# Tokens put in order by strided reads ahead of the first layer, and stores with 32 partitions as the outermost dimension

## The chip, the cores and the metric

The kernel runs on one core of one Trainium2 chip. The metric is the device time of one execution in microseconds (us). The engines are TensorE (PE in the rows; PEld is its weight load), VectorE (DVE), ScalarE (ACT), GpSimd (POOL) and SyncE (SP), whose queue issues most of the DMAs.

## What is computed

A causal convolution of 7 taps over the tokens, with softmaxed taps per head, and behind it two layers without attention: 192 to 2048 columns and back, with a squared ReLU in the first and a leaky ReLU in the second.

```python
def _attn_ref(x, weight):                      # x: 4 x 4096 x 192, weight: 8 heads x 7 taps
    ...
    w = np.exp(w)
    w = w / (np.sum(w, axis=-1, keepdims=True) + 1e-09)
    ...
    out = np.einsum('hk,bskhg->bshg', w, x_unf)
    return out.reshape(B, S, D)

def _moe_ref(x, w_in, w_out):                  # 16384 x 192, 192 x 2048, 2048 x 192
    h = x @ w_in
    r = np.maximum(h, 0.0)
    return (r * r) @ w_out

def _moe2_ref(x, w_in, w_out):
    h = x @ w_in
    return np.maximum(0.01 * h, h) @ w_out
```

## The kernel before

The 16384 tokens are cut into 32 tiles of TT = 512. A unit u = (l, t) is tile t in layer l; data stand with the 192 channels on partitions (a part "a" of 128 and a part "b" of 64) and the 512 tokens along the row. The units run in a fixed order: (1,0) to (1,3), (2,0), (2,1), and then alternately (2,t) and (1,t+2). Each unit has 8 steps. In a step TensorE makes two blocks of h (`g1`, from the operand x in X[u]) and, one step behind, multiplies the former step's blocks into the output o (`g2`). Every product is split into a high and a low part in fp32r for precision, so each block of h goes through ScalarE and VectorE: `act`, `most`, then `high` (line 385, ScalarE copy to fp32r) and `low` (line 389, VectorE subtraction), which make hi and lo, the moving operands of `g2`.

The operand x of a first-layer tile comes from the convolution. `load_x` (line 247) brings raw tokens from DRAM, `transpose` (line 267) turns blocks of 32 by 32, and `conv` sums the taps on VectorE into acc_a or acc_b in SBUF (lines 289 and 291); the first two tiles' part a is convolved on TensorE into PSUM (`conv_pe`, the name conv). Then four instructions split the result: `split_a` (line 326) and `split_b` (line 336) copy on ScalarE to the high part, `split_a_lo` (line 329) and `split_b_lo` (line 340) subtract on VectorE to the low part, and `copy_half` (line 320) copies halves between partitions with DMAs on SP's queue. The second layer's operand is split by the same four functions from the evacuated output z of layer one (`evac`, lines 425 to 433).

Each product (line 347) reads its moving operand in the order "p (a b) -> p b a" with a = 2: output column 2b + a is input column 256a + b. A tile passes four products, so its tokens stand in a turned order at the end: a column's 9-bit number has been rotated by 4 bits. The store undoes that. `store` (lines 447 to 457) transposes z in blocks of 32 by 32 into y_a or y_b and writes each group of 32 channels with one DMA of 512 runs of 32 floats (128 bytes), 65.5 KB. Its DRAM side has the order "(b i a) d -> a b i d" with b = 16, a = 2, so its outermost dimension has 2 elements, then 16, 16 and 32. The stores of all tiles go to SP's queue; for the last tile they alternate between SP's and ScalarE's.

What runs when is written out by hand (`tc.manual_schedule`). In each step `pieces` picks waiting instructions (the preparation of later tiles, the leaving of finished ones, the decoding of the int64-stored weights at lines 115 to 149) by due time and by a budget of costs in ns, which are constants in the code. On each engine the instructions then stay in that order. PSUM holds four blocks of h; X has four buffers, and the staging tiles w, y_a and y_b share three.

Of the kernel before, what the change touches and what calls it, by code (L numbers as in the profile page):

```python
# [31 lines left out]
def conv_moe_moe2_kernel(  # L32
# [20 lines left out]
    nc = tc.nc  # L53
# [21 lines left out]
    f32 = lambda ap: ap.bitcast(F32)  # L75
# [9 lines left out]
    for l in (1, 2):  # L85
        W[l] = dict(

            i=const.tile([P, NP, 3, 2, P], F32R, name=f"i{l}"),
# [218 lines left out]
    X, order, split = {}, [], set()  # L307

    def operand(u):
        if u not in X:  # L310
            X[u] = px.tile([P, 3, 2, TT], F32R, tag="x", name="x")
            order.append(u)
        return X[u]

    def room(u):

        return u in X or len(order) < XB or g1_left[order[len(order) - XB]] == 0

    def copy_half(u, k, to, k_from):
        nc.sync.dma_start(  # L320
            out=f32(X[u][halves(to), k].rearrange("p a t -> p (a t)")),
            in_=f32(X[u][halves(1 - to), k_from].rearrange("p a t -> p (a t)")),
        )

    def split_a(u, src):
        nc.scalar.copy(out=operand(u)[:, 0, 0, :], in_=src)  # L326

    def split_a_lo(u, src):
        nc.vector.tensor_sub(out=X[u][:, 0, 1, :], in0=src, in1=f32(X[u][:, 0, 0, :]))  # L329
        for i in range(2):  # L330
            copy_half(u, 1, i, 0)
        split.add(u)

    def split_b(u, src, half):
        v = halves(half)
        nc.scalar.copy(out=operand(u)[v, 2, 0, :], in_=src[v])  # L336

    def split_b_lo(u, src, half):
        v = halves(half)
        nc.vector.tensor_sub(out=X[u][v, 2, 1, :], in0=src[v], in1=f32(X[u][v, 2, 0, :]))  # L340
        copy_half(u, 2, 1 - half, 2)
        split.add(u)

# [73 lines left out]
    def evac(u):  # L417

        l, t = u
        o = ops.pop(u)  # L420
        z = {}

        def take(n, i):
            z[n, i] = pz.tile([P, HT], F32, tag="z", name="z")[:, 0:TT]
            (nc.vector.tensor_copy if i else nc.scalar.copy)(out=z[n, i], in_=o[n][i])  # L425

        def add(n):
            nc.vector.tensor_add(out=z[n, 0], in0=z[n, 0], in1=z[n, 1])  # L428
            if n == 1:
                nc.gpsimd.tensor_copy(out=z[1, 1][0:R], in_=z[1, 0][R:2 * R])  # L430

        def add_r():
            nc.vector.tensor_add(out=z[1, 0][0:R], in0=z[1, 0][0:R], in1=z[1, 1][0:R])  # L433

        now = [lambda n=n, i=i: take(n, i) for n in range(2) for i in range(2)]
        adds = [(690, lambda: add(1)), (690, lambda: add(0)), (690, add_r)]
        if l == 1:
            v = (2, t)
            free = lambda: room(v)
            return now, [z_ + (None,) for z_ in adds] + [  # L440
                (-600, lambda: split_a(v, z[0, 0]), free),
                (690, lambda: split_a_lo(v, z[0, 0]), free),
                (-600, lambda: split_b(v, z[1, 0], 0), free),
                (690, lambda: split_b_lo(v, z[1, 0], 0), free),
            ]

        def store(nm, src, n, dmas):
            y = stage.tile([P, TT], F32, tag="w", name=f"y_{nm}", bufs=WB)
            nc.vector.transpose(out=y[0:n], in_=src[0:n])
            d0 = 0 if nm == "a" else P  # L450

            for j in range(n // 32):
                to = out[t * TT:(t + 1) * TT, d0 + 32 * j:d0 + 32 * j + 32]
                dmas[j % len(dmas)].dma_start(  # L454
                    out=to.rearrange("(b i a) d -> a b i d", b=16, a=2),
                    in_=y[32 * j:32 * j + 32, :].rearrange("p (i d) -> p i d", d=32),
                )

        dmas = [nc.sync] if t < NT - 1 else [nc.sync, nc.scalar]
        both = adds + [  # L460
            (700, lambda: store("a", z[0, 0], P, dmas)),
            (700, lambda: store("b", z[1, 0], R, dmas)),
        ]
        if t == NT - 1:
            both = [both[i] for i in (1, 3, 0, 2, 4)]
        return now, [z_ + (None,) for z_ in both]
# [20 lines left out]
    with tc.manual_schedule():  # L487
# [67 lines left out]
        for i, (_, p) in enumerate(pieces):  # L555
            p()
            decode_ahead(400)
            if i == 2:
                xT1 = transpose_second()
        split_a((1, 0), acc0)  # L560
        split_a_lo((1, 0), acc0)
        split_b((1, 0), accb[0], 0)
        split_b_lo((1, 0), accb[0], 0)
        decode_ahead(10000)
        acc1 = conv_pe(xT1)

        def rest_of_second():
            split_b((1, 1), accb[0], 1)
            split_b_lo((1, 1), accb[0], 1)
            split_a((1, 1), acc1)  # L570
            split_a_lo((1, 1), acc1)
# [67 lines left out]
        for s in range(NS + 1):  # L639
            if s < NS:  # L640
                u, p = steps[s]
# [4 lines left out]
                if p == 0:  # L646
                    while u not in X or any(z[4] == u for z in list(prep) + list(leave)):
                        q = leave if any(z[4] == u for z in leave) else prep
                        z = q.popleft()
# [7 lines left out]
            if s:  # L657
                u2, p2 = steps[s - 1]
                g2(u2, p2)
                if p2 == NP - 1:  # L660
                    while leave:
                        z = leave.popleft()
# [76 lines left out]
```

## Time and profile before

| | us |
|---|---|
| median of 3 runs | 2244.81 (2244.11 to 2244.94) |
| profiled execution, its time | 2244.63 |
| profiled execution, its span | 2242.9 |
| TensorE busy | 2153.6 (96%) |
| VectorE busy | 1647.1 (73%) |
| ScalarE busy | 1657.9 (74%) |
| GpSimd busy | 83.7 (4%) |

The span is what the trace covers; the time of the execution is 1.73 us more. Busy times are sums over the instructions of an engine; a matmul's end is modelled, and weight loads run beside matmuls. In a row of a timeline the first number is the start in us from the span's start, the second the duration, and brackets hold the idle time before the instruction and what ended it. A DMA row on SPq or ACTq is the time for which the issuing queue was held, not the transfer.

### The profile page before, as it was taken

The page shows a single profiled execution, that of the slowest core. Times are in us where ns is not written, and L with a number is a line of the kernel's source. Part 1 is how long each engine was busy: PE and PEld are TensorE (multiplying, and loading weights), DVE is VectorE, ACT ScalarE, POOL GpSimd, SP SyncE. Part 2 cuts the span into 40 slices and gives each one's busy share as a digit, 9 for nine tenths or more (in the row PEclk, how much of TensorE's full clock was granted, in tenths as well). Part 3 has the DMA queues.
Part 4 walks back from the last instruction along what each step waited for, and adds up shares of the span by engine and source line. Part 5 has one row for each costly group of instructions (what it writes and reads, how often), then busy time and mean ns, then how long its engine had stood idle before and what let it go on. Part 6 is the DMA issues. An engine that isn't in the chain of part 4 may idle for free.

```text
span 2242.9 us, 47335 instructions
## 1 busy us (share of the span) xinstructions
PE 2153.6 (96%) x19488; PEld 1796.9 (80%) x19488; DVE 1647.1 (73%) x2633; ACT 1657.9 (74%) x2905; POOL 83.7 (4%) x148
## 2 busy tenths in 40 slices
PE   5698999999999999999999999999999999999995
PEld 3576888888888888888888888888888888888884
DVE  6778976777777786776777677687777768677655
ACT  4688667777777787777787777778777778777773
POOL 1000000000000000000000000000000000000000
PEclk9799999999999999999999999999999999999998
DMA  5333021211212121121221212122121212111111
GB/s 119 83 79 87 21 34 36 46 27 31 41 37 45 36 46 27 29 41 38 41 41 32 41 26 41 37 44 39 24 38 37 41 36 46 27 25 36 32 22 15
DMA packets 226889, 91.13 MB, mean 41 GB/s; under 512 B 204432, under 2 KB 214288, under 8 KB 226672
## 3 DMA queue, kind: packets, MB, share of 16 engines
q1 hardware_dynamic: 224250, 86.74, 19.9%
q8 instruction: 152, 2.49, 0.5%
q10 hardware_dynamic: 2230, 0.98, 0.2%
q0 software_dynamic: 192, 0.39, 0.1%
q14 instruction: 65, 0.53, 0.1%
HBM read 25.17 MB, written 12.58 MB: 17 GB/s over the span
## 4 chain that ended last, share of the span: by engine, by line
PE 63%; DVE 13%; ACT 12%; DMA 5%; issue 3%; SPq 1%; POOL 1%; DVEq 0%; POOLq 0%; ACTq 0%
PE o L347 33%; PE h L347 30%; DMA out_dram<-y_a 4%; ACT hi L385 4%; DVE lo L389 4%; ACT g L379 3%; ACT g L372 3%; DVE g L381 2%; DVE z L425 2%; POOL z L430 1%; SPq L454 1%; DVE z L433 1%; DVE z L428 1%; ACT x L326 1%; ACT x L336 1%
## 5 line engine op out<-in xcount | busy, mean ns | idle before, releaser
L347 PE MATMUL h<-x,i 64*128 64x512 f32 x9216 | 1086.7, 377 | 3.9 <-DMA x<-x 3.2
L347 PEld LDWEIGHTS h<-x,i 64*128 64x128 f32 x9216 | 879.1, 187 | 129.8 <-DMA x<-x 3.6
L347 PE MATMUL o<-hi,o 64*128 64x512 f32 x6144 | 869.5, 380 | 33.9 <-DVE o L149 26.9
L389 DVE TENSOR_TENSOR lo<-g,hi 128x512 fp32r<-128x512 f32 x1024 | 685.1, 689 | 280.0 <-ACT hi L385 252.1
L385 ACT CAST hi<-g 128x512 fp32r<-128x512 f32 x1024 | 628.8, 619 | 118.0 <-DVE g L381 101.8
L347 PEld LDWEIGHTS o<-hi,o 64*128 64x128 f32 x6144 | 586.2, 187 | 140.3 <-DVE o L149 30.1
L347 PE MATMUL o<-lo,o 64*128 64x512 f32 (+1 forms) x4096 | 632.7, 380 | 18.7 <-DVE lo L389 18.6
L381 DVE TENSOR_TENSOR g<-h,g 128x512 f32<-128x512 f32 x512 | 328.9, 683 | 185.2 <-ACT g L374 183.0
L347 PEld LDWEIGHTS o<-lo,o 64*128 64x128 f32 (+1 forms) x4096 | 334.9, 161 | 134.8 <-DVE lo L389 39.3
L374 ACT ACTIVATE g<-h 128x512 f32<-128x512 f32 x512 | 277.2, 593 | 214.4 <-PE h L347 214.2
L372 ACT ACTIVATE g<-h 128x512 f32<-128x512 f32 x512 | 303.9, 594 | 89.7 <-PE h L347 89.2
L379 ACT ACTIVATE g<-g 128x512 f32<-128x512 f32 x512 | 324.3, 633 | 13.9
L291 DVE SCALAR_TENSOR_TENSOR acc_a<-xT_a,taps,acc_a 128x512 f32<-128x512 f32 x180 | 133.9, 744 | 1.7
L430 POOL COPY z<-z 64x512 f32<-64x512 f32 x64 | 59.3, 926 | 1740.1 <-DVE z L428 1707.7
L428 DVE TENSOR_TENSOR z<-z 128x512 f32<-128x512 f32 x128 | 90.1, 733 | 1.6
L425 DVE COPY z<-o 128x512 f32<-128x512 f32 x128 | 82.0, 682 | 1.9 <-PE o L347 1.9
L291 DVE SCALAR_TENSOR_TENSOR acc_b<-xT_b,taps,acc_b 128x512 f32<-128x512 f32 x96 | 71.6, 746 | 1.1
L425 ACT COPY z<-o 128x512 f32<-128x512 f32 x128 | 68.3, 587 | 2.9 <-PE o L347 2.9
L326 ACT CAST x<-z 128x512 fp32r<-128x512 f32 x32 | 19.8, 617 | 63.5 <-DVE z L428 63.5
L433 DVE TENSOR_TENSOR z<-z 64x512 f32<-64x512 f32 x64 | 43.5, 680 | 17.4 <-POOL z L430 15.9
L340 DVE TENSOR_TENSOR x<-acc_b,x 64x512 fp32r<-64x512 f32 x32 | 22.0, 686 | 34.3 <-ACT x L336 34.2
L329 DVE TENSOR_TENSOR x<-acc_a,x 128x512 fp32r<-128x512 f32 x30 | 20.7, 689 | 29.7 <-ACT x L326 29.7
(65 smaller groups left out, 388.8 us busy)
## 6 DMA issues: line engine op xcount, KB each, us to landing
x<-x SPq DMA_DIRECT2D x192, 256.0 KB
raw_a<-in_x_dram SPq DMA_DIRECT2D x128, 64.0 KB
out_dram<-y_a SPq DMA_DIRECT2D x126, 64.0 KB
w<-in_moe_w_out_dram SPq DMA_DIRECT2D x15, 384.0 KB
raw_b<-in_x_dram SPq DMA_DIRECT2D x64, 64.0 KB
out_dram<-y_b SPq DMA_DIRECT2D x63, 64.0 KB
w<-in_moe_w_in_dram SPq DMA_DIRECT2D x14, 192.0 KB
w<-in_moe_w_in_dram SPq DMA_DIRECT2D x42, 64.0 KB
```

The source lines that it names most:

```text
L291: nc.vector.scalar_tensor_tensor(out=acc[0], in0=src, scalar=w, in1=acc[0], op0=ALU.mult, op1=ALU.add)
L347: nc.tensor.matmul(out=o.rearrange("p (b a) -> p b a", a=2), lhsT=w, rhs=z.rearrange("p (a b) -> p b a", a=2), start=begin, stop=end_,)
L372: nc.scalar.activation(out=g, in_=hps.pop((u, f)), func=ACTF.Relu)
L374: nc.scalar.mul(out=g, in_=hps[u, f], mul=0.01)
L379: nc.scalar.activation(out=g, in_=g, func=ACTF.Square)
L381: nc.vector.tensor_tensor(out=g, in0=hps.pop((u, f)), in1=g, op=ALU.max)
L385: nc.scalar.copy(out=a, in_=gsp[u, f])
L389: nc.vector.tensor_sub(out=b, in0=gsp.pop((u, f)), in1=f32(hi[u, f]))
L425: (nc.vector.tensor_copy if i else nc.scalar.copy)(out=z[n, i], in_=o[n][i])
L428: nc.vector.tensor_add(out=z[n, 0], in0=z[n, 0], in1=z[n, 1])
L430: nc.gpsimd.tensor_copy(out=z[1, 1][0:R], in_=z[1, 0][R:2 * R])
L433: nc.vector.tensor_add(out=z[1, 0][0:R], in0=z[1, 0][0:R], in1=z[1, 1][0:R])
```

## The change

Two things are changed together. Where a first-layer operand is made, the four splits read the convolution's result as "p (h l) -> p l h" with l = 16: consecutive elements of the read lie 16 floats (64 bytes) apart, and column 32l + h of the operand gets token 16h + l. Writes, and the second source of the subtractions, stay in order, in a view of 16 by 32; for the second layer both sides have that view, and the order is as before. After four products the tokens then stand in their natural order, and the store's DRAM side becomes "(i t) d -> t i d" with t = 32 outermost, then 16 and 32. The costs in the schedule are unchanged.

```diff
+    def taken(u, z):
+        return rows32(z) if u[0] == 2 else z.rearrange("p (h l) -> p l h", l=16)
+
+    rows32 = lambda z: z.rearrange("p (l h) -> p l h", l=16)
+
     def split_a(u, src):
-        nc.scalar.copy(out=operand(u)[:, 0, 0, :], in_=src)
+        nc.scalar.copy(out=rows32(operand(u)[:, 0, 0, :]), in_=taken(u, src))
 
     def split_a_lo(u, src):
-        nc.vector.tensor_sub(out=X[u][:, 0, 1, :], in0=src, in1=f32(X[u][:, 0, 0, :]))
+        nc.vector.tensor_sub(
+            out=rows32(X[u][:, 0, 1, :]), in0=taken(u, src), in1=rows32(f32(X[u][:, 0, 0, :]))
+        )
         for i in range(2):
             copy_half(u, 1, i, 0)
         split.add(u)
 
     def split_b(u, src, half):
         v = halves(half)
-        nc.scalar.copy(out=operand(u)[v, 2, 0, :], in_=src[v])
+        nc.scalar.copy(out=rows32(operand(u)[v, 2, 0, :]), in_=taken(u, src[v]))
 
     def split_b_lo(u, src, half):
         v = halves(half)
-        nc.vector.tensor_sub(out=X[u][v, 2, 1, :], in0=src[v], in1=f32(X[u][v, 2, 0, :]))
+        nc.vector.tensor_sub(
+            out=rows32(X[u][v, 2, 1, :]), in0=taken(u, src[v]), in1=rows32(f32(X[u][v, 2, 0, :]))
+        )
         copy_half(u, 2, 1 - half, 2)
         split.add(u)
...
                 dmas[j % len(dmas)].dma_start(
-                    out=to.rearrange("(b i a) d -> a b i d", b=16, a=2),
+                    out=to.rearrange("(i t) d -> t i d", t=32),
                     in_=y[32 * j:32 * j + 32, :].rearrange("p (i d) -> p i d", d=32),
                 )
```

## Rows read from the trace of the kernel before

**Rows 1.** The page's busy times, and its costliest group of matmuls.

```profile
PE 2153.6 (96%) x19488; PEld 1796.9 (80%) x19488; DVE 1647.1 (73%) x2633; ACT 1657.9 (74%) x2905; POOL 83.7 (4%) x148
...
L347 PE MATMUL h<-x,i 64*128 64x512 f32 x9216 | 1086.7, 377 | 3.9 <-DMA x<-x 3.2
```

**Rows 2.** Busy times by stage: the start, and a steady stretch.

```profile
core 0: us, PE busy (x) PEld busy (x) DVE busy (x) ACT busy (x) POOL busy (x), PEclk, DMA share, GB/s
20.00:240.00 220.00, 173.50 (x1335) 131.27 (x1335) 170.26 (x339) 163.11 (x303) 5.51 (x10) 0.91 0.34 85
...
700.00:1160.00 460.00, 457.24 (x4212) 385.28 (x4212) 337.29 (x522) 352.04 (x612) 15.86 (x25) 1.00 0.20 37
```

**Rows 3.** Timeline of the end: last matmuls, transposes of y, issues of stores.

```profile
2219.08 0.38 PE L347 MATMUL o<-hi,o 64*128 64x512 f32 x2
...
2221.02 0.71 DVE L449 STREAM_TRANSPOSE y_a<-z 128x512 f32<-128x512 f32 x1
...
2221.76 3.59 SPq L454 DMA_DIRECT2D out_dram<-y_a  x2
2221.77 5.48 ACTq L454 DMA_DIRECT2D out_dram<-y_a  x2
...
2223.80 0.70 DVE L449 STREAM_TRANSPOSE y_b<-z 64x512 f32<-64x512 f32 x1
2225.46 5.28 SPq L454 DMA_DIRECT2D out_dram<-y_b  x1
2227.34 6.42 ACTq L454 DMA_DIRECT2D out_dram<-y_b  x1
```

**Rows 4.** Slices by stage: a load of raw_b, then the last stores (columns as rows 2).

```profile
661.00:662.00 1.00, 1.00 (x12) 0.84 (x10) 0.32 (x1) 0.97 (x2) 0.00 (x0) 1.00 0.71 113
...
2223.00:2224.00 1.00, 0.00 (x0) 0.00 (x0) 0.89 (x2) 0.00 (x0) 0.05 (x1) 1.00 0.12 18
...
2226.00:2228.00 2.00, 0.00 (x0) 0.00 (x0) 0.00 (x0) 0.00 (x0) 0.00 (x0) 0.50 0.20 22
...
2240.00:2241.00 1.00, 0.00 (x0) 0.00 (x0) 0.00 (x0) 0.00 (x0) 0.00 (x0) 0.50 0.18 19
```

**Rows 5.** Line views: how long an issue holds its queue (ns, min/median/max).

```profile
L454 SPq DMA_DIRECT2D out_dram<-y_b x63: 2867/2957/5277, 286.9 to 2225.5; - x63
...
L247 SPq DMA_DIRECT2D raw_a<-in_x_dram x128: 311/486/742, 1.3 to 2000.2; - x128
```

**Rows 6.** Groups by line and shape: busy us, mean ns, then idle time before.

```profile
L127 DVE SCALAR_TENSOR_TENSOR m<-w,m 128x384 f32<-128x384 uint32 x32 | 18.9, 591 | 1.0
...
L149 DVE SCALAR_TENSOR_TENSOR i<-m,t 128x384 fp32r<-128x384 f32 x16 | 8.9, 558 | 0.5
L140 ACT CAST i<-t 128x384 fp32r<-128x384 f32 x16 | 8.2, 511 | 13.0 <-DVE t L134 12.9
...
L149 DVE SCALAR_TENSOR_TENSOR o<-m,t 128x256 fp32r<-128x256 f32 x16 | 6.8, 425 | 0.6
L140 ACT CAST o<-t 128x256 fp32r<-128x256 f32 x16 | 6.5, 404 | 9.6 <-DVE t L134 9.6
```

**Rows 7.** Timeline, first pattern of a first-layer split, and TensorE behind it.

```profile
611.71 0.61 ACT L326 CAST x<-acc_a 128x512 fp32r<-128x512 f32 x1
...
613.52 0.61 ACT L336 CAST x<-acc_b 64x512 fp32r<-64x512 f32 x1
...
614.17 0.69 DVE L340 TENSOR_TENSOR x<-acc_b,x 64x512 fp32r<-64x512 f32 x1 [0.53 <-ACT x L336]
...
615.64 0.65 PE L347 MATMUL o<-lo,o 64*64 64x512 f32 x4 [0.44 <-DVE lo L389]
```

**Rows 8.** Timeline, second pattern of a first-layer split, and TensorE behind it.

```profile
691.36 0.68 DVE L340 TENSOR_TENSOR x<-acc_b,x 64x512 fp32r<-64x512 f32 x1 [2.03 <-ACT x L336]
...
700.81 0.92 PE L347 MATMUL o<-hi,o 64*128 64x512 f32 x6 [0.16 <-ACT hi L385]
```

**Rows 9.** Timeline of the start: waits that end with DMAs.

```profile
29.70 5.10 PE L347 MATMUL h<-x,i 64*128 64x512 f32 x29 [3.25 <-DMA x<-x]
...
34.71 0.71 DVE L267 STREAM_TRANSPOSE xT_b<-raw_b 128x512 f32<-128x512 f32 x1 [4.72 <-DMA raw_b<-in_x_dram]
```

## The prediction

> **What bounds the kernel now.** I read the busy times first, then the same times by stage, then the waits and the two ends of the timeline. TensorE works 2153.6 us of the 2242.9 us span [rows 1]. In the steady stretch it is busy 457.2 of 460 us, while VectorE and ScalarE are busy 337 and 352 [rows 2]; so nothing is won there by a faster transfer or a shorter vector instruction, and something is lost only where a delay reaches TensorE. Two stretches are bound otherwise: from 20 to 240 us TensorE is busy 173.5 of 220 us [rows 2], and behind its last matmul, which ends at 2219.46, the span runs on for 23.4 us, most of it stores [rows 3].
>
> **The stores: what the new order of their dimensions takes away.** The last tile's six stores (four of y_a, two of y_b, 65.5 KB each) move at 22 GB/s with the DMA engines busy 0.20 of their time [rows 4], and each holds its issuing queue for about 3 us [rows 5]. The loads of raw_a and raw_b are cut into the same 512 runs of 128 bytes, but with 32 partitions outermost; they run at 113 GB/s with a share of 0.71 [rows 4], and hold the queue for 0.49 us [rows 5]. The stores get the loads' order. What a store's packet costs an engine is 0.20 x 16 engines / (22 GB/s / 128 B = 172 per us) = 18.6 ns, a load's 0.71 x 16 / 883 = 12.9 ns. With all 16 engines at the store's own price the rate is 16 x 128 B / 18.6 ns = 110 GB/s.
>
> In the tail: y_a is transposed by 2221.73, and the first packets move about 1.5 us later, since the slice from 2223 already has most of the steady rate [rows 3, 4]. The four y_a stores need 262 KB / 110 = 2.4 us, to 2225.6. y_b is ready at 2224.50, its packets start at 2226.0 and need 131 / 110 = 1.2 us, to 2227.2. Before, the last packet moves at about 2240.9 (the slice 2240 to 2241 is almost full [rows 4]), and the span ends 2.0 us later. So the tail ends at 2229.2, **13.7 us earlier**. Bounds: 14.1 us with the loads' packet price; 11 us if a store still held its queue for 2.96 us (SP would begin y_b at 2225.46 as now); nothing at all in a rival below. In the steady stretch the stores lie beside matmuls, and none of TensorE's waits there ends with a DMA (of its 3.9 us of idle time before the h matmuls 3.2 end with one [rows 1], and that wait lies at the start [rows 9]); the SP queue gets free sooner, so the x copies and raw loads queued behind the stores start sooner, which I cost at nothing: 2.8 us of 460 is all that TensorE has idle there [rows 2].
>
> The Trainium skill says in "DMA: Bandwidth & Descriptors" ("Why a DMA increments its semaphore by 16 and not by 1") that a transfer uses no more engines than divide its slowest dimension: 2 before, 16 after. Eight times 22 GB/s would be 176 GB/s and would take another 0.4 us off the tail; a share of 0.20 is more than two of sixteen engines can fill, so the trace agrees with "few engines", not with the exact two, and I keep 110 GB/s.
>
> **The strided reads: what the change adds.** For each of the 32 first-layer tiles, four instructions read one source with a step of 64 bytes: two ScalarE copies (lines 326 and 336) and two VectorE subtractions (lines 329 and 340). The second layer's splits read the same elements in the same order as before, in a view of 16 by 32: nothing. No row shows a step of 64 bytes, so the price p of one instruction is bounded. Low end: the decode reads int32 words with a step of 8 bytes; its two-source instruction on 384 elements takes 591 ns with one such source and 558 with none [rows 6], 33 ns, or 44 ns for 512. High end: that is 0.086 ns per element for one word skipped; at this price for 15 skipped words 1.29 ns per element, 0.66 us for 512. Between them lies one more pass per element: VectorE's slope is (558 - 425) / 128 = 1.04 ns, ScalarE's (511 - 404) / 128 = 0.84 ns [rows 6], so 0.53 and 0.43 us. Below nothing is excluded, since the same elements are read in a worse order. I take the pass more, 0.53 and 0.43: the step of 8 bytes already costs something though every second word is used, and here one in sixteen is. It is the least certain number of this prediction.
>
> By the Trainium skill, "Vector Engine (DVE) Microarchitecture Reference" (Measured stream behaviour on trn2), a source that hops at every element takes 1.73 ns a column instead of 1.05: 0.35 us for 512, as an estimate, and more for short steps; "SBUF — State Buffer" says that each change of a 16-byte line costs, without a price. With 0.35 for VectorE and my 0.43 for ScalarE the time would be 2268.6. The page's own wording, runs of two adjacent words, would also make the step of 8 bytes dear, and the trace shows 33 ns there, so its rule holds here at best from line to line.
>
> **Where these instructions lie.** They sit in ScalarE's and VectorE's queues in a fixed order, between the pieces that feed the second matmul. From the fifth tile on they come in two patterns, which take turns wherever I listed them (nine tiles between 420 and 960 us); over the 28 tiles that is 14 of each, and one of each is shown. In the first, ScalarE's copies start at 611.71 and 613.52 back to back with their neighbours, VectorE waits 0.53 us for the second, does line 340, and only then the subtraction lo, for which TensorE already waits 0.44 us [rows 7]. In the second, VectorE waits 2.03 us for the copy and then works without a gap into the evacuation, whose end TensorE meets with a wait of 0.16 us [rows 8]. Both chains have no slack left, so per tile 2 x 0.43 + 0.53 = 1.39 us reach TensorE (line 329 runs beside ScalarE's next work). 28 x 1.39 = **38.9 us**. At the start, the first tile's copy and two subtractions delay the transfers for which TensorE waits 3.25 us [rows 9]: 0.43 + 2 x 0.53 = 1.5 us. The second tile's splits are covered by VectorE's wait of 4.72 us for raw_b [rows 9]; without that cover they would cost the same again. Tiles three and four come while the engines are full: 2 x 1.39 = 2.8 us. Together 4.3 us.
>
> **Sum.** -13.7 + 38.9 + 4.3 = +29.5 us on the profiled execution: span 2242.9 to 2272.4, time 2244.63 to 2274.1. That execution lies 0.18 us under the median of 2244.81, so 2274.3. With equal p for all four instructions the cost is 28 x 3p + 9p = 93p, and the change breaks even at **p = 0.147 us**.
>
> **Rivals.** (1) The strided reads cost next to nothing and the tail's gain stays: at p = 44 ns, 4.1 us, so -9.6 and 2235.2; at nothing, 2231.1. For it speaks the small price of the 8-byte step [rows 6]; also TensorE reads its moving operand (line 347) by hops of 1 KB, at 377 ns for 512 columns with two matmuls in flight [rows 1]. Against it: another engine's path says little of these two, and 8 bytes is not 64. This one ends on the other side. (2) Only one engine pays. ScalarE alone: 28 x 0.86 + 0.43 + 1.72 - 13.7 = +12.5, 2257.3. VectorE alone: 28 x 0.53 + 1.06 + 1.06 - 13.7 = +3.3, 2248.1. (3) The change does not do what it says: 22 GB/s belongs to 128-byte writes and not to the order of dimensions. Then +43.2 with my p, 2288. Against it: a share of 0.20 means that most engines stand idle. (4) The step costs more than 0.66 us: 93 x 0.66 - 13.7 = +47.7, 2292.5, and more.
>
> **How the numbers follow.** Forecast 0.55, its own range 2259 to 2292 (p from 0.30 to 0.66); rival 1, 0.28; rival 2, 0.12 (ScalarE alone 0.07, VectorE alone 0.05); rival 3, 0.02; rival 4, 0.03. Since both signs carry weight, the range for 8 in 10 runs from 2231 to 2290, and leaves out rival 4, the top of the forecast's range and the very bottom of rival 1. About 0.2% (4.5 us) is what a measurement of this kernel can tell from no change: faster 0.28, same 0.05 (VectorE alone), slower 0.67.
>
> **What would show it.** The means of lines 326, 329, 336 and 340 on the convolution's results against those on z: +0.43 and +0.53 us are the forecast, under 0.15 is rival 1. Stores that hold their queue for about 0.6 us and a tail of about 9.7 us behind the last matmul show the first part. TensorE's wait for lo in the first kind of tile should grow from 0.44 to about 1.8 us, and a steady pair of tiles by 2.8 us. It is wrong if the strided reads are cheap, or if they are dear and TensorE still does not wait.

## The result and the profile after

The changed kernel takes 2266.91 us (median of 4 runs, 2265.76 to 2268.41) against 2244.88 before: 1.0100 times as long, with a 95% interval of 1.0084 to 1.0116. The interval leaves out 1: the change loses, if only 1%. In the profiled executions the span goes from 2242.9 to 2264.8 us, +21.9. Two places account for all of it. The last matmul ends 36.7 us later (2256.17 instead of 2219.46), and the tail behind it is 14.8 us shorter (8.6 instead of 23.4 us).

The groups by line and shape show what the step of 64 bytes costs. Lines 326, 329, 336 and 340 are now 333, 336, 345 and 349; columns are those of [rows 6]. First before, then after:

```profile
L340 DVE TENSOR_TENSOR x<-acc_b,x 64x512 fp32r<-64x512 f32 x32 | 22.0, 686 | 34.3 <-ACT x L336 34.2
...
L329 DVE TENSOR_TENSOR x<-acc_a,x 128x512 fp32r<-128x512 f32 x30 | 20.7, 689 | 29.7 <-ACT x L326 29.7
...
L336 ACT CAST x<-acc_b 64x512 fp32r<-64x512 f32 x32 | 19.5, 610 | 0.4
...
L326 ACT CAST x<-acc_a 128x512 fp32r<-128x512 f32 x30 | 18.3, 611 | 2.0 <-DVE acc_a L291 2.0
...
L329 DVE TENSOR_TENSOR x<-conv,x 128x512 fp32r<-128x512 f32 x2 | 1.4, 692 | 1.1 <-ACT x L326 1.1
...
L326 ACT CAST x<-conv 128x512 fp32r<-128x512 f32 x2 | 1.2, 582 | 0.0
```

```profile
L345 ACT CAST x<-acc_b 64x512 fp32r<-64x512 f32 x32 | 34.4, 1075 | 0.4
L349 DVE TENSOR_TENSOR x<-acc_b,x 64x512 fp32r<-64x512 f32 x32 | 33.4, 1043 | 38.7 <-ACT x L345 38.7
L333 ACT CAST x<-acc_a 128x512 fp32r<-128x512 f32 x30 | 32.6, 1088 | 1.6 <-DVE acc_a L291 1.6
L336 DVE TENSOR_TENSOR x<-acc_a,x 128x512 fp32r<-128x512 f32 x30 | 32.1, 1070 | 41.7 <-ACT x L333 41.7
...
L336 DVE TENSOR_TENSOR x<-conv,x 128x512 fp32r<-128x512 f32 x2 | 1.4, 692 | 1.1 <-ACT x L333 1.1
...
L333 ACT CAST x<-conv 128x512 fp32r<-128x512 f32 x2 | 1.2, 582 | 0.0
```

So a ScalarE copy got 0.47 to 0.48 us longer and a VectorE subtraction 0.36 to 0.38 us. The second layer's copies of part a (x<-z) took 617 ns before and 618 after. Nor did part a of the two tiles whose convolution lies in PSUM (x<-conv) change: 582 and 692 ns, as before, though it too is read with the step of 64 bytes.

The timeline of TensorE, from 600 to 740 us, shows where this arrives; brackets are its idle time. They answer to [rows 7, 8].

```profile
621.48 0.65 PE L358 MATMUL o<-lo,o 64*64 64x512 f32 x4 [0.45 <-DVE lo L400]
623.85 0.65 PE L358 MATMUL o<-lo,o 64*64 64x512 f32 x4 [1.08 <-DVE lo L400]
702.22 0.65 PE L358 MATMUL o<-lo,o 64*64 64x512 f32 x4 [0.91 <-DVE lo L400]
710.32 0.92 PE L358 MATMUL o<-hi,o 64*128 64x512 f32 x6 [0.34 <-ACT hi L396]
```

The instruction that stood at 615.64 stands at 623.85 (+8.21), the one at 700.81 at 710.32 (+9.51): one tile more, 1.30 us more. That is 2 x 0.47 + 0.36. In the first pattern it arrives as two waits for lo, 0.45 and 1.08 us, where one of 0.44 stood. In the second most of it arrives at 702.22, at a wait for lo of 0.91 us that did not exist before, and little at the wait for hi that the prediction named (0.34 us for 0.16). The waits view sums up TensorE's waits for lo (us in total, times, longest), before and after:

```profile
PE o L347 <- DVE lo L389: 18.6, 27, 1.8
...
PE o L358 <- DVE lo L400: 47.6, 57, 1.8
```

The end of the timeline, and slices of it (columns as in [rows 2]), answer to [rows 3, 4]:

```profile
2255.79 0.38 PE L358 MATMUL o<-hi,o 64*128 64x512 f32 x2
...
2258.47 0.85 SPq L464 DMA_DIRECT2D out_dram<-y_a  x2
...
2261.23 0.32 SPq L464 DMA_DIRECT2D out_dram<-y_b  x1
2261.24 0.37 ACTq L464 DMA_DIRECT2D out_dram<-y_b  x1
```

```profile
2260.00:2261.00 1.00, 0.00 (x0) 0.00 (x0) 0.96 (x2) 0.00 (x0) 0.00 (x0) 0.57 0.99 142
...
2262.00:2263.00 1.00, 0.00 (x0) 0.00 (x0) 0.00 (x0) 0.00 (x0) 0.00 (x0) 0.50 0.80 121
```

A store of y_b now holds its queue for 0.32 and 0.37 us instead of 5.28 and 6.42 [rows 3], and the stores move at up to 142 GB/s with the DMA engines busy 0.99 of the time, where it was 22 GB/s at 0.20.

### The profile page after: what moved, and what is told of

It reads as the page before. It is cut to its first block, busy times and chain, and to the rows that moved or that the text cites. A ratio compares the mean times of both kernels' runs of the same rounds, so it can differ in the third digit from the quotient of the medians.

```text
span 2264.8 us, 47335 instructions
## 1 busy us (share of the span) xinstructions
PE 2159.3 (95%) x19488; PEld 1794.7 (79%) x19488; DVE 1671.9 (74%) x2633; ACT 1686.0 (74%) x2905; POOL 83.5 (4%) x148
## 4 chain that ended last, share of the span: by engine, by line
PE 65%; DVE 15%; ACT 14%; issue 4%; POOL 1%; DMA 1%; SPq 0%; ACTq 0%; POOLq 0%; DVEq 0%
PE o L358 34%; PE h L358 31%; DVE lo L400 4%; ACT hi L396 4%; ACT g L390 3%; ACT g L383 3%; DVE acc_a L291 2%; DVE g L392 2%; DVE z L436 2%; ACT x L333 1%; ACT x L345 1%; POOL z L441 1%; DVE z L444 1%; DVE z L439 1%; DVE t L134 1%
## 5 line engine op out<-in xcount | busy, mean ns | idle before, releaser
L390 ACT ACTIVATE g<-g 128x512 f32<-128x512 f32 x512 | 324.7, 634 | 13.8
L336 DVE TENSOR_TENSOR x<-acc_a,x 128x512 fp32r<-128x512 f32 x30 | 32.1, 1070 | 41.7 <-ACT x L333 41.7
L349 DVE TENSOR_TENSOR x<-acc_b,x 64x512 fp32r<-64x512 f32 x32 | 33.4, 1043 | 38.7 <-ACT x L345 38.7
```

Of the source, the lines that this page charges most:

```text
L390: nc.scalar.activation(out=g, in_=g, func=ACTF.Square)
```

## The experiments

**The two parts apart.** The first kernel has the new stores alone, the second the strided reads alone.

```diff
 # e1_stores_only: before, with
-                    out=to.rearrange("(b i a) d -> a b i d", b=16, a=2),
+                    out=to.rearrange("(i t) d -> t i d", t=32),
 # e2_reads_only: the changed kernel, with
-                    out=to.rearrange("(i t) d -> t i d", t=32),
+                    out=to.rearrange("(b i a) d -> a b i d", b=16, a=2),
```

> Only the store's new order of dimensions; the splits read in order as before, so the tokens of a tile come out in a turned order. Theory (stores and strided reads are two separate terms; the stores' gain lies in the tail alone): the matmuls end at 2219.5 as before, the tail behind them falls from 23.4 to 8.6 us, time 2230.0. Rival (part of the 36.7 us by which the last matmul came later stems from the faster stores, which meet the x copies or the raw loads in the DMA engines): the matmuls end more than 2 us later than 2219.5, time above 2232.

> Only the strided reads, with the old stores, so the tokens of a tile come out in a turned order. Theory: the four strided instructions alone move the last matmul by 36.7 us, the tail stays 23.4 us: time 2244.9 + 36.7 = 2281.6. Rival (the two parts act on each other): below 2279 or above 2284.

Stores alone: 2229.51 us, 0.9936 of before (0.9919 to 0.9952). Reads alone: 2281.44 us, 1.0168 (1.0153 to 1.0184). Against the 2243.67 us of before on the same chip that is -14.2 and +37.8, together +23.6, where the change as a whole had +22.0 (on another chip). In the profiled executions, whose spans are 2227.8 and 2279.8 us, it is -15.1 and +36.9, together +21.8 for +21.9. The ends of the two timelines say that each part acts in its own place; first e1, then e2:

```profile
2218.78 0.38 PE L347 MATMUL o<-hi,o 64*128 64x512 f32 x2
...
2224.23 0.38 ACTq L454 DMA_DIRECT2D out_dram<-y_b  x1
```

```profile
2256.03 0.38 PE L358 MATMUL o<-hi,o 64*128 64x512 f32 x2
...
2264.28 6.41 ACTq L464 DMA_DIRECT2D out_dram<-y_b  x1
```

With the stores alone the last matmul ends at 2219.16, 0.3 us from before: a tail of 8.6 us. With the reads alone it ends at 2256.41, as in the changed kernel (2256.17): the tail of 23.4 us is the old one. The faster stores cost nothing in the steady stretch, and the strided reads are the whole of the loss.

**Which of the four instructions reach TensorE.** One engine's reads are strided, the other's in order, with the old stores.

```diff
 # e6_scalar_only: the changed kernel, old stores, and
-            ... in0=taken(u, src), in1=rows32(f32(X[u][:, 0, 0, :]))
+            ... in0=rows32(src), in1=rows32(f32(X[u][:, 0, 0, :]))
 # e7_vector_only: the changed kernel, old stores, and
-        nc.scalar.copy(out=rows32(operand(u)[:, 0, 0, :]), in_=taken(u, src))
+        nc.scalar.copy(out=operand(u)[:, 0, 0, :], in_=src)
 # in both, the same for part b
```

> Old stores; only the two ScalarE copies read with the step of 64 bytes, the VectorE subtractions read in order (so the low part is not that of the high part, and the output is another one). Theory (no slack behind the splits: each tile adds the sum of its chain, 27 tiles): 2 x 0.47 us per tile, 27 x 0.94 + 1 = 26.4, time 2271. Rival (half of it is covered by VectorE's waits, or only the longest of the instructions counts): 0.47 us per tile, 2258.

> Old stores; only the two VectorE subtractions read with the step of 64 bytes, the ScalarE copies in order (the output is another one). Theory: line 340's extra 0.36 us reaches TensorE in each tile, line 329's is covered: 27 x 0.36 + 0.5 = 10.2, time 2255. Rival (both subtractions count): 27 x 0.74 = 20, time 2265; rival (VectorE's waits for ScalarE cover it): 2245.

ScalarE alone: 2271.10 us, 1.0123 (1.0106 to 1.0140), its last matmul at 2246.16, +26.7. VectorE alone: 2254.19 us, 1.0048 (1.0033 to 1.0063), last matmul at 2230.16, +10.7. In e6 the subtraction takes its difference from what ScalarE wrote, so the two parts still sum to the convolution's result. Only how it is split differs, and not, as the expectation had it, what is computed. Both numbers are those of the theory (26.4 and 10.2 from the chain's sum), and 26.7 + 10.7 = 37.4 is close to the 37.0 of both together (e2). Of VectorE's two subtractions only one counts per tile, 0.36 us and not 0.74. The wait in front of the second shows which one is free:

```profile
L349 DVE TENSOR_TENSOR x<-acc_b,x 64x512 fp32r<-64x512 f32 x32 | 33.7, 1054 | 24.2 <-ACT x L345 23.3
```

VectorE's idle time before line 349 (340 before) falls from 34.3 to 24.2 us. That is about what line 336 (329 before) got longer in 30 tiles, 30 x 0.37 = 11 us: while ScalarE still makes the copy of part b, VectorE would have waited anyway.

**How the price depends on the step.** Only part a is read with a step, another in each pair of tiles.

```diff
+    FORMS = [   # (how the source is read, how operand and high part are walked)
+        (lambda z: z.rearrange("p (h l) -> p l h", l=2), lambda z: z.rearrange("p (l h) -> p l h", l=2)),
...             # the same with l = 4, 8, 128
+        (lambda z: z.rearrange("p (h l w) -> p l h w", l=8, w=2), lambda z: z.rearrange("p (l h w) -> p l h w", l=8, w=2)),
...             # and in order
+            nc.scalar.copy(out=FORMS[0][1](o), in_=FORMS[0][0](src))      # a line for each form
```

> Old stores; only part a of the first layer's splits (lines of split_a and split_a_lo) reads with steps that change from pair of tiles to pair of tiles: 2, 4, 8 and 128 elements, pairs of neighbours 16 apart, and none (the output is another one). Theory (a line of 16 bytes is what a read pays for): step 2 and pairs cost nothing or little (under 0.1 us), steps 4, 8 and 128 cost as the step of 16 did, 0.47 us on ScalarE and 0.38 us on VectorE. Rival 1 (the price grows with the words skipped, as the prediction's upper bound had it): 0.1 at step 4, 0.2 at 8, 0.47 at 16, over 1 us at 128. Rival 2 (only neighbouring pairs are free): step 2 costs as much as 16.

The groups of e8 (one execution, 2256.24 us), ScalarE's lines 339 to 349 and VectorE's 357 to 367, each in the order of 2, 4, 8, 128, pairs, in order:

```profile
L341 ACT CAST x<-acc_a 128x512 fp32r<-128x512 f32 x6 | 9.1, 1517 | 0.6 <-DVE acc_a L291 0.6
L359 DVE TENSOR_TENSOR x<-acc_a,x 128x512 fp32r<-128x512 f32 x6 | 8.1, 1343 | 10.8 <-ACT x L341 10.8
L343 ACT CAST x<-acc_a 128x512 fp32r<-128x512 f32 x6 | 6.8, 1129 | 1.4 <-DVE acc_a L291 1.4
L345 ACT CAST x<-acc_a 128x512 fp32r<-128x512 f32 x6 | 6.6, 1103 | 0.0
L361 DVE TENSOR_TENSOR x<-acc_a,x 128x512 fp32r<-128x512 f32 x6 | 6.6, 1103 | 9.3 <-ACT x L343 9.3
L363 DVE TENSOR_TENSOR x<-acc_a,x 128x512 fp32r<-128x512 f32 x6 | 6.5, 1088 | 8.3 <-ACT x L345 8.3
L339 ACT CAST x<-acc_a 128x512 fp32r<-128x512 f32 x4 | 3.4, 854 | 0.0
L357 DVE TENSOR_TENSOR x<-acc_a,x 128x512 fp32r<-128x512 f32 x4 | 3.3, 828 | 4.5 <-ACT x L339 4.4
L367 DVE TENSOR_TENSOR x<-acc_a,x 128x512 fp32r<-128x512 f32 x4 | 2.8, 689 | 3.9 <-ACT x L349 3.9
L365 DVE TENSOR_TENSOR x<-acc_a,x 128x512 fp32r<-128x512 f32 x4 | 2.8, 689 | 3.9 <-ACT x L347 3.9
L347 ACT CAST x<-acc_a 128x512 fp32r<-128x512 f32 x4 | 2.5, 634 | 0.0
L349 ACT CAST x<-acc_a 128x512 fp32r<-128x512 f32 x4 | 2.4, 610 | 0.0
```

Against the order (610 and 689 ns), step 2 costs 0.24 us on ScalarE and 0.14 on VectorE, step 4 0.91 and 0.65, step 8 0.52 and 0.41, step 128 0.49 and 0.40; 16 had 0.48 and 0.38 in the changed kernel. Pairs of neighbours that lie 16 elements apart cost 0.02 and nothing. The price does not grow with the words skipped, so the prediction's upper bound had no ground; a hop at each element costs about 0.5 us on ScalarE and 0.4 on VectorE at each length measured from 8 elements on, and a hop after each second element next to nothing. Why 4 elements are the dearest stays open. The Trainium skill, "Vector Engine (DVE) Microarchitecture Reference" (Measured stream behaviour on trn2), has this for VectorE: free in runs of two adjacent words, 1.73 ns a column with one source hopping at each element (here 1.04 + 0.38 / 0.512 = 1.78), more for small steps than for large ones. The trace agrees at step 4, the dearest, and disagrees at the smallest: single words at step 2 cost VectorE 0.14 us here, less than any longer step measured, and 33 ns in [rows 6].

**A strided read that is free.** The order is made where the second layer's output leaves PSUM, by the same step of 64 bytes; new stores, splits in order.

```diff
 # e3_order_at_evac: before, with the new stores and, in evac's take,
+            src, dst = o[n][i], z[n, i]
+            if l == 2:
+                src, dst = src.rearrange("p (k b) -> p b k", b=16), dst.rearrange("p (b k) -> p b k", b=16)
-            (nc.vector.tensor_copy if i else nc.scalar.copy)(out=z[n, i], in_=o[n][i])
+            (nc.vector.tensor_copy if i else nc.scalar.copy)(out=dst, in_=src)
```

> The new stores, but the tokens are put in order where the second layer's output is copied out of PSUM, by a read with a step of 64 bytes; the splits read in order. Theory (a step of 64 bytes costs nothing on a source in PSUM, as the two tiles convolved by TensorE showed: 582 ns and 692 ns before and after): the copies stay at 587 and 682 ns, time 2230. Rival (it was the small number of tiles; a strided read costs about 0.47 us on ScalarE and 0.36 us on VectorE from PSUM too): copies of 1060 and 1040 ns; two of each per tile stand in the evacuation, so up to 31 tiles x 1 us come on top: 2235 to 2260.

2229.17 us, 0.9935 of before (0.9920 to 0.9950). The copies of both layers stand in one group each; half of them are strided, and the means are those of before. First before, then e3:

```profile
L425 DVE COPY z<-o 128x512 f32<-128x512 f32 x128 | 82.0, 682 | 1.9 <-PE o L347 1.9
...
L425 ACT COPY z<-o 128x512 f32<-128x512 f32 x128 | 68.3, 587 | 2.9 <-PE o L347 2.9
```

```profile
L428 DVE COPY z<-o 128x512 f32<-128x512 f32 x128 | 82.0, 681 | 0.8 <-PE o L347 0.8
...
L428 ACT COPY z<-o 128x512 f32<-128x512 f32 x128 | 68.2, 586 | 1.6 <-PE o L347 1.6
```

So the step costs neither engine anything on a source in PSUM, and this kernel has the whole gain of the stores without the loss.

**The same order at TensorE.** The first product of the first layer reads its moving operand so that the tokens come out in order.

```diff
 # e5_order_at_pe: before, with the new stores and, for g1 of the first layer,
-            out=o.rearrange("p (b a) -> p b a", a=2), lhsT=w, rhs=z.rearrange("p (a b) -> p b a", a=2),
+                out=o.rearrange("p (c h a) -> p c h a", c=8, a=2), lhsT=w,
+                rhs=z.rearrange("p (h a c) -> p c h a", a=2, c=8), start=begin, stop=end_,
```

> The new stores, the splits read in order, and TensorE puts the tokens in order: in the first product of the first layer the moving operand is read with hops of 8 columns (32 bytes) and more instead of 256 columns (1 KB). Theory (TensorE reads by hops at no cost, as it already does at 1 KB): h matmuls of the first layer stay at 377 ns, time 2230. Rival (short hops cost TensorE as they cost VectorE and ScalarE): 32 tiles x 8 steps x 18 matmuls, in pairs of 216 ns; at one column in two passes 32 x 8 x 9 x 0.216 = 498 us more, time about 2730.

2677.72 us, 1.1934 (1.1916 to 1.1952). The first layer's h matmuls (line 348) as a group, and a step of them in the timeline:

```profile
L348 PE MATMUL h<-x,i 64*128 64x512 f32 x4608 | 1039.5, 607 | 4.6 <-DMA x<-x 2.6 <-DVE i L149 1.9
...
917.28 4.05 PE L348 MATMUL h<-x,i 64*128 64x512 f32 x18
```

The mean was 377 ns before [rows 1], and is 376 for the second layer's here. A step's 18 matmuls take 4.05 us where they took 2.11, so the rival held in most of its size: 449 us over e3, which has the same new stores, of the 498 expected. TensorE, too, pays for hops of 8 columns. The old order does not: it alternates between two streams 1 KB apart, each read in order. Whether the alternation or the length of the hop makes the difference was not tried.

**Why the old stores were slow.** First their outermost dimension is cut away: each is split by a into two transfers with 16 partitions outermost, and neither addresses nor tokens move.

```diff
 # e4_two_stores: before, with
-                dmas[j % len(dmas)].dma_start(
-                    out=to.rearrange("(b i a) d -> a b i d", b=16, a=2),
-                    in_=y[32 * j:32 * j + 32, :].rearrange("p (i d) -> p i d", d=32),
-                )
+                for a in range(2):
+                    dmas[j % len(dmas)].dma_start(
+                        out=to.rearrange("(b i a) d -> a b i d", b=16, a=2)[a],
+                        in_=y[32 * j + 16 * a:32 * j + 16 * a + 16, :].rearrange("p (i d) -> p i d", d=32),
+                    )
```

> Before, with each store cut into two by its outermost dimension a: two transfers of 256 runs with 16 partitions outermost, to the same addresses of DRAM in the same turned order. Theory (few elements in the outermost dimension keep a store on few DMA engines): each holds its queue for about 0.3 us, the tail falls to about 9 us, time 2230.5. Rival (the old order of addresses, neighbouring runs 2 tokens apart instead of 32, is what is slow): stores stay at 22 GB/s, tail 23 us, time 2245.

2229.91 us, 0.9938 (0.9924 to 0.9953). The end of its timeline:

```profile
2217.54 0.38 PE L347 MATMUL o<-hi,o 64*128 64x512 f32 x2
...
2222.98 1.23 SPq L455 DMA_DIRECT2D out_dram<-y_b  x2
```

Each half holds its queue for about 0.6 us, more than expected, so a pair costs 1.2 us of issuing; the last matmul ends at 2217.92 in a span of 2227.5, a tail of 9.6 us. The order of the addresses was not what was slow.

Then the size itself, in one kernel: 4, 8 and 16 elements outermost in three of four tiles, 2 in the fourth.

```diff
 # e9_outermost: before, with four forms of
-                    out=to.rearrange("(b i a) d -> a b i d", b=16, a=2),
+                    q.dma_start(out=to.rearrange("(b i a) d -> a b i d", b=8, a=4), in_=src_y)   # b=4, a=8; b=2, a=16; b=16, a=2
```

> Before, but the stores' outermost dimension has 4, 8 or 16 elements in tiles 0, 1 and 2 of each four, and 2 as before in the fourth and so in the last tile (the same runs of 128 bytes and the same number; the tokens of the first three come out in another order). Theory (the number of elements in the outermost dimension is the number of DMA engines that work): a store holds its queue, once the queue is full, for 2.96 us at 2, about 1.5 at 4, 0.75 at 8 and 0.5 at 16, and the rate goes from 22 to 44, 88 and over 100 GB/s; the time stays at 2244, since the last tile has the old stores. Rival (a threshold: all but 16 or 32 are as slow as 2): 2.96 us at 4 and 8 too.

The issues of y_b on SP's queue (457 has 4 outermost, 459 has 8, 461 has 16, 463 has 2), the issues of y_a with 8 (ns, min/median/max), and a slice of a store with 4, one with 8 and one with 16:

```profile
1746.71 5.99 SPq L463 DMA_DIRECT2D out_dram<-y_b  x2
...
1799.20 2.89 SPq L457 DMA_DIRECT2D out_dram<-y_b  x2
...
1873.60 1.40 SPq L459 DMA_DIRECT2D out_dram<-y_b  x2
...
1930.79 1.25 SPq L461 DMA_DIRECT2D out_dram<-y_b  x2
```

```profile
L459 SPq DMA_DIRECT2D out_dram<-y_a x32: 675/704/782, 303.4 to 2129.1; - x32
```

```profile
1800.00:1801.00 1.00, 1.00 (x12) 0.82 (x12) 0.85 (x2) 0.97 (x2) 0.00 (x0) 1.00 0.40 43
...
1873.00:1874.00 1.00, 1.00 (x12) 0.86 (x10) 0.75 (x2) 0.62 (x2) 0.00 (x0) 1.00 0.67 112
...
1929.00:1930.00 1.00, 1.00 (x14) 0.87 (x12) 1.00 (x3) 0.97 (x3) 0.00 (x0) 1.00 0.64 103
```

Per store of y_b that is 3.0, 1.45, 0.70 and 0.63 us for 2, 4, 8 and 16; 65.5 KB in these times are 22, 45, 94 and 104 GB/s. From 2 over 4 to 8 the rate doubles each time, and at 16 it stops. But at 8 all issues of y_a, the first of a tile too, which finds the queue empty, hold it for 0.68 to 0.78 us, about as long as a store of y_b. So from 8 on the issuing sets the rate, and these rates do not say what the DMA engines could do.

The packet records of the traces point to how many work. Beside its 512 packets of 128 bytes a store leaves packets of 4 bytes: the six stores of a tile leave 12 with 2 elements outermost, 24 with 4, 48 with 8, 96 with 16, and 96 again with the changed kernel's 32. That is 2, 4, 8, 16 and 16 per store. Of the 128-byte packets no more than 4 are ever in flight at once with 2 elements outermost, and no more than 8 with 4. By the rule that the Trainium skill gives in "DMA: Bandwidth & Descriptors" ("Why a DMA increments its semaphore by 16 and not by 1"), a transfer runs on as many engines, up to 16, as divide its slowest dimensions, and each of them ends with one write to the semaphore. The counts agree, if the 4-byte packets are these writes.

The time, 2243.43 us (one execution; 2244.90 for before on the same chip), is that of before, as the last tile has the old form.

## Why the prediction came out as it did

The direction, both mechanisms and their places were right: the time grew, through slower instructions in a chain without slack, less a shorter tail. The sum was too high, +29.5 us on the profiled execution against +21.9. Its terms:

| term | predicted | measured |
|---|---|---|
| tail | -13.7 | -14.8 |
| start (to the last wait before 240 us) | +4.3 | +1.7 |
| steady stretch | +38.9 (28 x 1.39) | +35.0 (27 x 1.30) |
| sum | +29.5 | +21.9 |

- **Tail.** Right, 1.1 us too careful: the rate was up to 142 GB/s and not 110, and the issue of y_b 0.3 to 0.4 us and not 0.6. The 110 rested on a misreading. The share of 0.20 was taken for busy engines, 3.2 of 16, and so for a price of 18.6 ns a packet on an engine. But it counts the time of packets, and they overlap: in the old tail 2 to 4 are in flight at once. So the share does not speak against two engines, as the prediction had it, and the 4-byte packets point to two. That 110 came so near is in part luck.
- **Price p.** "The least certain number" came out between the bounds and near the pass more: ScalarE 0.47 to 0.48 for 0.43, VectorE 0.36 to 0.38 for 0.53. VectorE's was the mis-sized term; the 0.35 us worked out from the Trainium skill's figure was nearer. The two errors cancel in part, which is luck: over 28 tiles ScalarE's two copies cost 2.2 us more than forecast and VectorE's subtraction 4.8 us less. The reason given for the high side, a price for each word skipped, was wrong: e8 shows no such growth.
- **No slack behind the splits.** Right to a few hundredths of a us in 27 tiles, 1.30 against 2 x 0.47 + 0.36, and e6 and e7 show that the terms add one by one. The prediction's sentence that line 329 does not count was right as well.
- **How many tiles.** The shift by 240 us was 1.71 us (230.71 against 229.00 for the wait before the h blocks run freely), and (36.71 - 1.71) / 1.30 = 26.9: one tile of the 28 does not pay. It is the fifth, the first of the 28, at about 285 us; matmul by matmul, TensorE is 1.72 us late ahead of its splits and 1.72 us behind them, and each of the 27 later tiles adds 1.27 to 1.32. The nine tiles that the prediction listed all lie later. At the fifth the step in work is one of the second layer (line 374, now 385), where ScalarE waits long for h, and this wait takes in the delay; before and after:

```profile
290.29 1.09 ACT L374 ACTIVATE g<-h 128x512 f32<-128x512 f32 x2 [1.52 <-PE h L347]
...
292.00 1.09 ACT L385 ACTIVATE g<-h 128x512 f32<-128x512 f32 x2 [0.33 <-PE h L358]
```

- **The start.** The term that failed. Of its 4.3 us, 1.5 were for the first tile, whose part a comes from PSUM and costs nothing more (582 and 692 ns). The prediction had no bound for PSUM apart from SBUF, though the two sources stood in groups of their own before. Part b comes from SBUF and did get slower, but TensorE's wait for the x copies [rows 9] ended at 29.23 us instead of 29.70, and at 29.29 in e1, which has no strided reads: the first tile's 1.5 us did not come. At the last wait before 240 us the reads alone (e2) stand 2.0 us behind before and the stores alone (e1) 0.2 us ahead; how the 2.0 divides between tiles three and four, for which 2.8 were forecast, stays open. The first wait in the changed kernel:

```profile
29.23 6.16 PE L358 MATMUL h<-x,i 64*128 64x512 f32 x29 [2.53 <-DMA x<-x]
```

- **Rival 1** fell with the price of the step from SBUF, not with its logic: where the strided read is free (e3), the time is 2229.2, close to its 2231.1. The rate of TensorE was no argument for it; e5 shows that TensorE pays for hops of 8 columns, and that the 1 KB in the trace was not the same thing.

## What to carry to other kernels

A reorder was free here where ScalarE or VectorE read it from PSUM, and nearly so where it moved pairs of neighbours; the same step from SBUF cost 0.36 to 0.48 us for 512 elements. What such a delay costs is told by the chain behind it: on engines three quarters busy 1.30 us a tile arrived at TensorE whole, because an instruction that TensorE waits for stood behind it in the queue. A store's outermost dimension is worth a look before its tokens are moved: cutting each store in two (e4) gave 13.8 us, with no reorder at all, where the new order of dimensions alone (e1) gave 14.2.

## What the runs showed of the hardware that I had not expected

- A step of 64 bytes costs ScalarE and VectorE nothing on a source in PSUM (582, 586, 692 and 681 ns) and 0.36 to 0.48 us on one in SBUF.
- A step of 4 elements (16 bytes) in SBUF is dearer than 8, 16 and 128: 1517 ns on ScalarE, 1343 on VectorE, against 1088 and 1070 at 16 elements.
- A moving operand in hops of 8 columns takes TensorE 4.05 us for 18 matmuls instead of 2.11; the 2.11 are those of two alternating streams 1 KB apart.
- A store's rate followed its outermost dimension: 22, 45 and 94 GB/s at 2, 4 and 8 elements, the last limited by the issuing. So did its packets of 4 bytes: 2, 4, 8 and 16 per store at 2, 4, 8 and 16 elements, and 16 at 32.
